# Block products with seven multiplications in the channel mixer of an attention-and-mixer kernel

## The chip, the cores and the metric

The kernel runs on one core of a Trainium2 chip. The core has a matrix engine (TensorE, PE in the profile), a vector engine (VectorE, DVE), a scalar engine (ScalarE, ACT), a general engine (GpSimd, POOL) and a queue engine (SyncE, SP), 16 DMA engines, an on-chip memory of 128 partitions (SBUF) and eight accumulator banks (PSUM). PEld is TensorE's loading of the stationary operand, which overlaps its matmuls. The metric is the device time of one execution in microseconds. Three runs of the kernel before took 810.48, 810.80 and 811.31 us; the median is 810.8.

## What is computed

Eight batches go through attention in chunks of 64 rows and then through a mixer with a token part and a channel part. Cut to what matters:

```python
B, H, S, D = 8, 8, 576, 64                     # chunk = 64
scores = scale * q_c @ k_c.transpose            # 64 x 64 for each of 9 chunks, 8 heads
attn = exp(scores - max) ; attn = attn / (sum(attn) + 1e-9)
x = (attn @ v_c) laid out as (B, 576, 512)
# mixer, for each batch
h = relu(x.T @ w_tok1) @ w_tok2                 # 512 x 576 -> 512 x 256 -> 512 x 576
u = x + h.T
out = u + relu(u @ w_ch1) @ w_ch2               # 576 x 512 -> 576 x 1536 -> 576 x 512
```

All of it is in float32. TensorE takes a rounded form of it (float32r). To keep the precision, every operand is split into a high part (rounded) and a low part (the value less its rounded form), and every product is computed as three: high by high, low by high and high by low (`THREE` in the code).

## The kernel before

The batches are numbered b = 0 to 7. Attention works on tiles of 128 rows (two chunks), 36 in all; a batch with even b has five tiles, one with odd b four (the middle tile of nine is shared by two batches). The mixer works with the channel dimension (512 = 4 blocks of 128, `NDT`) on partitions and the 576 rows of the sequence as two halves of 288 columns (`HALF`), n = 0 and 1. The hidden channels are 12 blocks of 128 (`NFC`).

For one batch the work is:

- `tok1` (L499): the first token product, two blocks of 128 (`NT1`), 14 matmuls of 512 columns each (`tok1_part`, L476). Then relu on ACT (rh, L493) and the low part on DVE (rl, L494).
- `tok2` (L505): the second token product, 2 halves x 4 blocks x 6 = 48 matmuls of 288 columns (L514), each block followed by the addition of x on DVE (L519), the rounding on ACT (L524) and the low part on DVE or POOL (L525).
- `ch1` (L529): the first channel product of a half n and a block f: 4 x 3 = 12 matmuls (L535), then relu on ACT (gh, L544) and the low part on DVE (gl, L545).
- `ch2` (L559): the second channel product of that block, 4 x 3 = 12 matmuls (L575) into four accumulators that stay in PSUM for all 12 blocks. After the last one DVE adds u's high part (L582), POOL its low part (L584), and SP stores the result.
- One attention interruption (`attention`, L747): the scores of one tile and the values of the tile before it, 64 matmuls of 64x64 (`attn_both`, L309 and L321), into one pair of PSUM banks. Then DVE takes the maximum (mx, L282), subtracts (pr, L285), ACT takes exp (L289), DVE transposes (L332), SP sends the result to DRAM and back in another order (far and pf, `far_out` and `far_in`), and ACT copies it (pt, L360) for the next interruption. DVE also sums the rows (L295) and multiplies the values by the reciprocals (x, L400); ACT and POOL split x (xh, xl, L417 and L418); x is transposed and goes through DRAM too (xt), to be added in `tok2`.

The order on TensorE is written out by hand from b = 1 on (`manual_schedule` for the tensor engine): in 24 steps (n, f) `ch1` of a step, then `ch2` of the step before it. `LAST_STEP` and `STRIDE` say in which steps an attention interrupts. On ACT, DVE and POOL a planner orders the instructions with its own costs; SP is in program order. In batch 0 the planner orders TensorE as well: there DVE and ACT turn the weights, which arrive as 64-bit floats, into float32 (`conversion`) and split them, `STEP_FILL` operations a step. The attention of batch 1's four tiles runs in batch 0, in the slots of `STARTS`: the scores of a tile in one slot, its values three slots later, the next tile after that. The scores of batch 2's first tile (tile 9) stand alone at step 0 of batch 1. At the end of batch 0 and of every later one the two blocks of `tok1` for the next batch stand beside the last two `ch2` steps.

PSUM holds four accumulators (`ps_acc`), two banks for `ch1` and `tok1` (`ps_c1`) and one pair for attention (`ps_at`).

## Time and profile before

| what | value |
|---|---|
| median of three runs | 810.8 us |
| the profiled execution, its own time | 810.02 us |
| its span in the profile | 808.2 us |
| TensorE busy | 787.4 us, 97% |
| DVE, ACT, POOL busy | 378.0, 240.7, 118.5 us |
| moved by DMA | 87.96 MB, mean 109 GB/s |
| granted TensorE clock, mean | 0.992 |

Batch 0 ends (the second token product of b = 1 begins) at about 150 us; later batches begin at 247.8, 342.1, 437.7, 532.0, 627.6 and 721.5 us.

How to read the profile: the page gives busy times by engine, then the span in 40 slices of 20.2 us with the busy share in tenths, then the chain of waits that ended last, then groups of instructions by line, engine, operation and tile with their count, busy time and mean duration in ns, and the idle time before them with what ended it. A tile name such as `gl<-ps_c,gh` reads output, then inputs. L545 is line 545 of the kernel before.

### The profile page before, as it was taken

The numbers are of one execution on the slowest core, as the hardware profiler recorded it, in microseconds if no ns is written. First come the engines' busy times: TensorE is split into PE (matmuls) and PEld (weight loads), VectorE is DVE, ScalarE is ACT, GpSimd is POOL, SyncE is SP. The second block draws the span as 40 slices with busy tenths as digits, with TensorE's granted clock in tenths as the row PEclk, the third lists the DMA queues.
The fourth block names the chain that finished last, engine by engine and source line by source line (L and its number), as shares of the span: only waits on it lengthen the run. The fifth ranks groups of instructions, "written<-read, shape, count | busy, mean of one in ns | idle before, by whom it ended". The sixth has DMA issues, their size and how long they took to land.

```text
span 808.2 us, 17939 instructions
## 1 busy us (share of the span) xinstructions
PE 787.4 (97%) x7556; PEld 752.1 (93%) x7556; DVE 378.0 (47%) x799; ACT 240.7 (30%) x496; POOL 118.5 (15%) x137
## 2 busy tenths in 40 slices
PE   7889999899999999999999999999999999999997
PEld 5579989799999999999999999999999999999997
DVE  5989985545344344253534334344533445232111
ACT  4667643322232222132223222222223222121111
POOL 0000120401203021130203102030200302033000
PEclk8999999999999999999999999999999999999999
DMA  9953322344432233123441234222342223200000
GB/s 349 406 190 105 119 79 96 135 122 141 148 112 64 92 122 107 56 79 125 141 151 58 64 115 140 88 70 93 131 145 89 76 88 101 67 30 1 1 30 30
DMA packets 69985, 87.96 MB, mean 109 GB/s; under 512 B 8016, under 2 KB 48208, under 8 KB 69904
## 3 DMA queue, kind: packets, MB, share of 16 engines
q1 hardware_dynamic: 69904, 86.82, 32.5%
q8 instruction: 59, 0.97, 0.5%
q14 instruction: 22, 0.18, 0.1%
HBM read 59.92 MB, written 25.95 MB: 106 GB/s over the span
## 4 chain that ended last, share of the span: by engine, by line
PE 85%; DVE 8%; DMA 3%; ACT 2%; issue 1%; SPq 0%; ACTq 0%; DVEq 0%
PE acc L575 36%; PE ps_c L535 33%; PE ps_t L476 6%; PE ps_t L514 6%; PE ps_sv L309 2%; PE ps_sv L321 2%; DVE wtop L173 1%; DVE wtop L181 1%; DMA xc<-x 1%; DVE kept_c L231 1%; DVE wtop L160 1%; DMA raw_t<-in_w 1%; DMA pf<-far 1%; DVE wtop L166 1%; PE sum L485 0%
## 5 line engine op out<-in xcount | busy, mean ns | idle before, releaser
L535 PE MATMUL ps_c<-uh,kept_c 128*128 128x288 f32 x1536 | 310.8, 295 | 3.4 <-ACT xt L447 1.9
L575 PE MATMUL acc<-gh,kept_c 128*128 128x288 f32 x1536 | 311.9, 299 | 1.6 <-ACT kept_c L225 1.1
L535 PEld LDWEIGHTS ps_c<-uh,kept_c 128*128 128x128 f32 x1536 | 245.8, 188 | 4.8 <-ACT xt L447 2.1
L575 PEld LDWEIGHTS acc<-gh,kept_c 128*128 128x128 f32 x1536 | 244.2, 188 | 6.4 <-ACT kept_c L225 1.8
L535 PE MATMUL ps_c<-ul,kept_c 128*128 128x288 f32 x768 | 226.6, 295 | 0.0
L545 DVE SCALAR_TENSOR_TENSOR gl<-ps_c,gh 128x288 fp32r<-128x288 f32 x180 | 81.4, 452 | 310.1 <-ACT gh L544 309.9
L575 PE MATMUL acc<-gl,kept_c 128*128 128x288 f32 x768 | 219.5, 295 | 0.0
L544 ACT ACTIVATE gh<-ps_c 128x288 fp32r<-128x288 f32 x180 | 74.1, 411 | 317.1 <-PE ps_c L535 316.6
L535 PEld LDWEIGHTS ps_c<-ul,kept_c 128*128 128x128 f32 x768 | 144.2, 188 | 0.1
L575 PEld LDWEIGHTS acc<-gl,kept_c 128*128 128x128 f32 x768 | 142.9, 189 | 0.1
L418 POOL TENSOR_TENSOR xl<-x,xh 128x512 fp32r<-128x512 f32 x28 | 38.3, 1366 | 413.0 <-ACT xh L417 413.0
L584 POOL TENSOR_TENSOR o<-o,ul 128x288 f32<-128x288 f32 x56 | 44.1, 813 | 192.7 <-DVE o L582 191.1
L514 PE MATMUL ps_t<-kept_t,rh 128*128 128x288 f32 x224 | 44.7, 295 | 0.3 <-ACT rh L493 0.3
L289 ACT ACTIVATE pr<-pr 128x512 f32<-128x512 f32 x36 | 22.7, 632 | 61.6 <-DVE pr L285 59.9
L582 DVE TENSOR_TENSOR o<-acc,uh 128x288 f32<-128x288 f32 x56 | 22.7, 448 | 36.1 <-PE acc L575 31.5
L476 PE MATMUL ps_t<-xh,kept_t 128*128 128x512 f32 x112 | 36.0, 405 | 2.5 <-ACT xh L417 2.5
L524 ACT CAST uh<-u 128x288 fp32r<-128x288 f32 x64 | 27.1, 433 | 37.6 <-DVE u L519 37.6
L360 ACT COPY pt<-pf 128x512 f32<-128x512 f32 x31 | 19.2, 620 | 60.3 <-DMA pf<-far 60.3
L514 PEld LDWEIGHTS ps_t<-kept_t,rh 128*128 128x128 f32 x224 | 35.9, 188 | 1.0 <-ACT rh L493 1.0
L514 PE MATMUL ps_t<-kept_t,rl 128*128 128x288 f32 x112 | 33.2, 297 | 0.2 <-DVE rl L494 0.2
L519 DVE TENSOR_TENSOR u<-ps_t,xt 128x288 f32<-128x288 f32 x64 | 28.4, 452 | 9.8 <-PE ps_t L514 9.4
L525 POOL TENSOR_TENSOR ul<-u,uh 128x288 fp32r<-128x288 f32 x35 | 29.1, 848 | 10.0 <-ACT uh L524 9.5
(79 smaller groups left out, 629.4 us busy)
## 6 DMA issues: line engine op xcount, KB each, us to landing
qk<-in_qk SPq DMA_DIRECT2D x36, 512.0 KB, 3.9
far<-blocks SPq DMA_DIRECT2D x63, 256.0 KB, 2.1
raw_c<-in_wc SPq DMA_DIRECT2D x24, 512.0 KB, 9.0
v<-in_v SPq DMA_DIRECT2D x36, 260.0 KB, 4.1
out<-o SPq DMA_DIRECT2D x64, 144.0 KB, 1.9
pf<-far SPq DMA_DIRECT2D x124, 64.0 KB, 2.0
xt<-far SPq DMA_DIRECT2D x112, 64.0 KB, 2.0
raw_t<-in_w SPq DMA_DIRECT2D x4, 288.0 KB, 7.9
```

The source lines that it names most:

```text
L289: nc.scalar.activation(out=pr, in_=pr, func=AF.Exp, scale=1.0 / float(D) ** 0.5)
L418: nc.gpsimd.tensor_tensor(out=xl, in0=t["x"], in1=xh.bitcast(F32), op=ALU.subtract)
L476: nc.tensor.matmul(ps, lhsT=lhsT, rhs=rhs, start=(n == 0 and q == 0), stop=(n == len(mt) - 1 and q == len(terms) - 1),)
L514: nc.tensor.matmul(ps[:, :HALF], lhsT=lhsT[:, m * P:(m + 1) * P], rhs=rhs, start=(k == 0 and q == 0), stop=(k == NT1 - 1 and q == len(term ...
L519: nc.vector.tensor_tensor(out=u.rearrange("p (i c) -> p i c", c=BK), in0=ps[:, :HALF].rearrange("p (i c) -> p i c", c=BK), in1=xt[:, n * H ...
L524: nc.scalar.copy(out=uh[:, m], in_=u)
L525: return lambda engine: engine.tensor_tensor(out=ul[:, m], in0=u, in1=uh[:, m].bitcast(F32), op=ALU.subtract)
L535: nc.tensor.matmul(ps[:, :HALF], lhsT=weights["c1", f][:, wi, k * P:(k + 1) * P], rhs=u[ui][:, k], start=(k == 0 and q == 0), stop=(k == N ...
L544: nc.scalar.activation(out=gh, in_=ps[:, :HALF], func=AF.Relu)
L545: nc.vector.scalar_tensor_tensor(out=gl, in0=ps[:, :HALF], scalar=0.0, in1=gh.bitcast(F32), op0=ALU.max, op1=ALU.subtract)
L575: nc.tensor.matmul(accs[e], lhsT=weights["c2", f][:, wi, e * P:(e + 1) * P], rhs=g[gi], start=(f == 0 and q == 0), stop=(f == NFC - 1 and ...
L584: nc.gpsimd.tensor_tensor(out=o, in0=o, in1=u[1][:, e].bitcast(F32), op=ALU.add)
```

## The change

From b = 2 on the first channel product is no longer computed block by block. Two blocks of hidden channels, two halves of the input channels and two halves of the sequence make a 2x2 by 2x2 block product. It is computed with seven block products in place of eight (Winograd's form of Strassen's method): sums of the weight blocks (S1 to S4) and of the blocks of u (T1 to T4) are multiplied, and the results are sums of the seven products (`seven`). Six such pairs (`NPAIR`) make a batch.

The sums of weights don't change from batch to batch. They are made once in batch 1 (`make`, in the steps `MAKE`), split, and written to DRAM together with the plain blocks (`send`, two steps later). Every pair of every batch from b = 2 on loads its seven blocks from DRAM (`load`), on ACT's DMA queue, in two transfers into doubled buffers. The sums of u are made in each batch from the second token product (`operands`); their high parts come from ACT, their low parts from DVE or, for three of them, POOL.

Both halves of the sequence come out of a pair together. The first half goes into `ch2` at once, in the next pair; the second half is kept in SBUF (`store`) and runs as 12 `ch2` steps when the pairs are done. The first token product of the next batch stands before the last three of these steps (`TOKEN_1`), and the last two steps (`TOKEN_2`) are kept back: one runs after the next batch's second token product, one after the first two products of its first pair.

PSUM: from b = 2 on the banks of `ps_c1` and `ps_at` become one pool of four (`ps_mix`), from which token products, block products and attention all take their tiles in turn. Attention takes two of them, so its DVE operations come in two halves.

The attention of batch 1's tiles in batch 0 also takes the merged form, scores of a tile with values of the tile before, in five slots; tile 9's scores move into the last of them. In batch 1 the attention stands before `ch1`, and the steps are 4, 8, 12, 16 and 20. From b = 2 on it stands where `BREAKS` says. The weights of the token products become slices of two tiles (`wtall` and `kept_t`), and batch 0's kept relu results one tile. The output addition of b = 2 to 7 needs one DVE operation in place of one on DVE and one on POOL, as u is kept whole.

The diff, cut to its core:

```diff
+SEVEN = (
+    ("A11", "B11"), ("A12", "B21"), ("S2", "T2"), ("S1", "T1"), ("S4", "B22"), ("S3", "T3"), ("A22", "T4"),
+)
+GROUP = 4
+NPAIR = NFC // 2
+BREAKS = {
+    5: (("pair", 0), ("pair", 2), ("pair", 4), ("mid", 5), ("step", 4)),
+    4: (("pair", 1), ("pair", 3), ("pair", 5), ("step", 3)),
+}
+TOKEN_1, TOKEN_2 = 8, 10
+LOW_ON_GPSIMD = {"B21", "B22", "T3"}
+MAKE = (1, 5, 9, 13, 17, 20)
+SEND = 2
+FIRST_LOADS = (21, 23)
-LAST_STEP, STRIDE, FIRST_STEP = 19, {5: 4, 4: 5}, 0
+LAST_STEP, STRIDE = 20, 4
-STARTS = ((8, 9, 11, 12), (13, 14, 16, 17), (18, 19, 21, 22), (23, 24, 26, 27))
+STARTS = (10, 14, 18, 22, 26)
...
+    def tok1_pair(b, cover):
+        src, tag = (ps_mix[0], "c") if mixing else (ps_c1, "c1")
+        ps = []
+        for m in range(NT1):
+            ps.append(src.tile([P, 512], F32, tag=tag, name="ps_t1"))
+            for n in range(NKT - 1):
+                tok1_part(b, m, n, ps[m])
+            if m == 0:
+                cover()
+        for m in range(NT1):
+            tok1_part(b, m, NKT - 1, ps[m])
+        return [tok1_end(x) for x in ps]
...
+    def make(p):
+        full = pool.tile([P, 2, DM], F32, tag="full", name="full", bufs=1)
+        for i in range(2):
+            w = weights["c1", 2 * p + i]
+            nc.gpsimd.tensor_tensor(
+                out=full[:, i], in0=w[:, 0].bitcast(F32), in1=w[:, 1].bitcast(F32), op=ALU.add
+            )
...
+        for i, x, op, y in (
+            (1, a21, ALU.add, a22), (0, sums[:, 1], ALU.subtract, a11),
+            (2, a12, ALU.subtract, sums[:, 0]), (3, a11, ALU.subtract, a21),
+        ):
+            nc.vector.tensor_tensor(out=sums[:, i], in0=x, in1=y, op=op)
+        parts = pool.tile([P, 4, 2, DM // 2], F32R, tag="wparts", name="wparts", bufs=1)
+        nc.scalar.copy(out=parts[:, :, 0], in_=sums)
+        nc.vector.tensor_tensor(
+            out=parts[:, :, 1], in0=sums, in1=parts[:, :, 0].bitcast(F32), op=ALU.subtract
+        )
+        return parts
+    def send(p, parts):
...
+        for at, src in ((0, a1[:, 0]), (1, a1[:, 1]), (slice(2, 6), parts.bitcast(F32)), (6, a2[:, 1])):
+            nc.scalar.dma_start(out=mixed[p][:, at], in_=src)
+    def load():
+        if loads:
+            src = mixed[loads.pop(0)]
+            got = []
+            for tag, lo, hi in (("mwa", 0, GROUP), ("mwb", GROUP, len(SEVEN))):
+                w = pool.tile([P, hi - lo, 2, DM // 2], F32R, tag=tag, name=tag)
+                nc.scalar.dma_start(out=w.bitcast(F32), in_=src[:, lo:hi])
+                got += [w[:, i] for i in range(hi - lo)]
+            loaded.append(got)
...
+    def operands(b, r):
...
+        def add(name, src):
+            full[name] = src
+            high, low = [every[:, len(ops), i] for i in range(2)]
+            nc.scalar.copy(out=high, in_=src)
+            engine = nc.gpsimd if name in LOW_ON_GPSIMD else nc.vector
+            engine.tensor_tensor(out=low, in0=src, in1=high.bitcast(F32), op=ALU.subtract)
+            ops[name] = (high, low)
+        def minus(name, x, y):
+            t = pool.tile([P, 2, HALF], F32, tag="diff", name="diff", bufs=2)
+            nc.vector.tensor_tensor(out=t, in0=full[x], in1=full[y], op=ALU.subtract)
+            add(name, t)
...
+        minus("T2", "B22", "T1")
+        minus("T3", "B22", "B12")
+        minus("T4", "B21", "T2")
+    def seven(p, ops, w, store, between, interrupt):
+        def run(i):
+            ps = ps_mix[0].tile([P, 512], F32, tag="c", name="ps_m")[:, :HALF]
+            for k in range(2):
+                for q, (wi, ui) in enumerate(THREE):
+                    nc.tensor.matmul(
+                        ps, lhsT=w[i][:, wi, k * P:(k + 1) * P], rhs=ops[SEVEN[i][1]][ui][:, k],
+                        start=(k == 0 and q == 0), stop=(k == 1 and q == 2),
+                    )
+            return ps
+        m1 = half("m1")
+        nc.scalar.copy(out=m1, in_=run(0))
+        first = relu_split(plus(half("c11"), run(1), m1))
+        interrupt("mid", p)
+        between(0)
+        u2 = plus(half("u2"), run(2), m1)
+        u4 = plus(half("u4"), run(3), u2)
+        between(1)
+        plus(store[:, 2 * p], run(4), u4)
+        m7 = run(5)
+        u3 = plus(half("u3"), m7, u2)
+        plus(store[:, 2 * p + 1], m7, u4)
+        second = relu_split(plus(half("c21"), run(6), u3))
+        return first, second
...
+    for b in range(2, B):
+        u, ops = operands(b, r)
+        rest.pop(0)()
...
+        def between(k):
+            if todo:
+                ch2(b, 0, u[0], *todo[k], accs)
+            elif k == 0:
+                rest.pop(0)()
+        for p in range(NPAIR):
+            interrupt("pair", p)
+            first, second = seven(p, ops, loaded.pop(0), store, between, interrupt)
+            load()
+            todo = [(2 * p, first), (2 * p + 1, second)]
+        for f, g in todo:
+            ch2(b, 0, u[0], f, g, accs)
+        accs, ahead, rest = [], relu_split(store[:, 0]), []
+        for f in range(NFC):
+            interrupt("step", f)
+            g, ahead = ahead, None
+            if b + 1 < B and f >= TOKEN_2:
+                g = g or relu_split(store[:, f])
+                rest.append(lambda b=b, f=f, g=g, u=u[1], accs=accs: ch2(b, 1, u, f, g, accs))
+            else:
+                if b + 1 < B and f == TOKEN_1:
+                    r = tok1_pair(b + 1, lambda: ch2(b, 1, u[1], f, g, accs))
+                else:
+                    ch2(b, 1, u[1], f, g, accs)
+                ahead = relu_split(store[:, f + 1]) if f + 1 < NFC else None
```

`half` takes a buffer of 288 columns, `plus` adds a PSUM tile and an SBUF tile on DVE, and `relu_split` takes relu on ACT (high part) and the low part on DVE.

More of the change, by code (lines that the diff above doesn't have):

```diff
@@ L120, in attention_mixer_kernel @@
     plan += [(("t2", k, n), w2_in, k * S + n * HALF, HALF) for n in range(2) for k in range(NT1)]
-    token = len(plan)
+    token, token_words = len(plan), sum(p[3] for p in plan)
     for f in range(-1, NFC):
@@ L222, in split_high @@
         name = "kept_" + "_".join(map(str, key))
-        kept = ctx.enter_context(tc.tile_pool(name=name, bufs=1, reuse_waits="tile"))
-        parts = tops[key, "parts"] = kept.tile([P, 2, n], F32R, name=name)
+        if i < token:
+            if "kept_t" not in weights:
+                weights["kept_t"] = const.tile([P, 2 * token_words + 2 * DT], F32R, name="kept_t")
+            at = 2 * sum(p[3] for p in plan[:i])
+            parts = weights["kept_t"][:, at:at + 2 * n].rearrange("p (w n) -> p w n", w=2)
+        else:
+            kept = ctx.enter_context(tc.tile_pool(name=name, bufs=1, reuse_waits="tile"))
+            parts = kept.tile([P, 2, n], F32R, name=name)
+        tops[key, "parts"] = parts
         nc.scalar.copy(out=parts[:, 0], in_=tops[i])
@@ L301, in attn_both @@
     def attn_both(i, j):
-        ps = ps_at.tile([P, 2, 512], F32, tag="at", name="ps_sv")
+        if mixing:
+            ps = [ps_mix[0].tile([P, 512], F32, tag="c", name="ps_sv") for _ in range(2)]
+        else:
+            pair = ps_at.tile([P, 2, 512], F32, tag="at", name="ps_sv")
+            ps = [pair[:, a] for a in range(2)]
         if i is not None:
@@ new lines, in make @@
+    def make(p):
[5 more added lines that the diff above has]
+            )
+        (a11, a12), (a21, a22) = [[full[:, i, h * DM // 2:(h + 1) * DM // 2] for h in range(2)] for i in range(2)]
+        sums = pool.tile([P, 4, DM // 2], F32, tag="wsum", name="wsum", bufs=1)
+        for i, x, op, y in (
[5 more added lines that the diff above has]
+        nc.scalar.copy(out=parts[:, :, 0], in_=sums)
+        nc.vector.tensor_tensor(
+            out=parts[:, :, 1], in0=sums, in1=parts[:, :, 0].bitcast(F32), op=ALU.subtract
+        )
+        return parts
@@ new lines, in later @@
+    def later(job, *args):
+        with tc.issue_after([i for i in nc.cur_bb.bb.instructions if i.engine == nc.scalar.engine][-1]):
+            job(*args)
+    done = len(STARTS)
+    us = []
+    for n in range(2):
+        uh = pool.tile([P, NDT, HALF], F32R, tag="uh", name="uh")
+        ul = pool.tile([P, NDT, HALF], F32R, tag="ul", name="ul")
+        us.append((uh, ul))
+        for m in range(NDT):
+            tok2(1, r, n, m, us[n])(nc.vector if n * NDT + m in UL_ON_VECTOR else nc.gpsimd)
@@ new lines, in attention_mixer_kernel @@
+    ends = len(batch_tiles(2))
+    steps = {LAST_STEP - STRIDE * k for k in range(ends)}
+    made, pend = [], None
+    for n in range(2):
+        accs = []
+        for f in range(NFC):
+            step = n * NFC + f
+            if step in steps:
+                attention(done)
+                done += 1
+            g = ch1(us[n], f)
+            if step in MAKE:
+                with ExitStack() as late:
+                    newest = {i.engine: i for i in nc.cur_bb.bb.instructions}
+                    for engine in (nc.scalar.engine, nc.vector.engine):
+                        late.enter_context(tc.issue_after(newest[engine]))
+                    made.append((step + SEND, MAKE.index(step), make(MAKE.index(step))))
+            if made and made[0][0] == step:
+                later(send, *made.pop(0)[1:])
+            if step in FIRST_LOADS:
+                later(load)
+            if step == 2 * NFC - 2:
+                held = pend
+            elif step == 2 * NFC - 1:
+                rest = [pend, (1, n, us[n], f, g, accs)]
+                r = tok1_pair(2, lambda: None)
+                ch2(*held)
+            elif pend is not None:
+                ch2(*pend)
+            pend = (1, n, us[n], f, g, accs)
@@ new lines, in half, with plus, relu_split @@
+    def half(name, bufs=2):
+        return pool.tile([P, HALF], F32, tag=name, name=name, bufs=bufs)
+    def plus(dst, ps, other):
+        nc.vector.tensor_tensor(out=dst, in0=ps, in1=other, op=ALU.add)
+        return dst
+    def relu_split(src):
+        gh, gl = g_parts()
+        nc.scalar.activation(out=gh, in_=src, func=AF.Relu)
+        nc.vector.scalar_tensor_tensor(
+            out=gl, in0=src, scalar=0.0, in1=gh.bitcast(F32), op0=ALU.max, op1=ALU.subtract
+        )
+        return gh, gl
```

237 lines of the change are left out of this document (127 added, 110 removed).

## The prediction

> **What bounds the kernel now.** I read the page first, then the windows by stage, then what TensorE waited for.
>
> ```profile
> span 808.2 us, 17939 instructions
> PE 787.4 (97%) x7556; PEld 752.1 (93%) x7556; DVE 378.0 (47%) x799; ACT 240.7 (30%) x496; POOL 118.5 (15%) x137
> DVE  5989985545344344253534334344533445232111
> ```
> ```profile
> 60.00:80.00 20.00, 20.00 (x173) 19.31 (x172) 20.00 (x43) 15.20 (x30) 0.00 (x0) 1.00 0.31 106
> 247.80:342.10 94.30, 94.30 (x910) 92.11 (x910) 36.70 (x78) 21.87 (x46) 15.55 (x18) 1.00 0.30 93
> 342.10:437.70 95.60, 95.60 (x975) 93.19 (x974) 42.34 (x88) 25.44 (x52) 15.65 (x18) 1.00 0.35 112
> ```
> ```profile
> PE ps_sv L321 <- ACT pt L360: 0.5, 1, 0.5
> PE ps_t L514 <- ACT rh L493: 0.3, 1, 0.3
> PE ps_t L514 <- DVE rl L494: 0.2, 1, 0.2
> ```
>
> In a window row the columns are PE, PEld, DVE, ACT and POOL busy, granted clock, DMA share and GB/s. The batches called b = 2 and b = 3 in the code (windows two and three) keep TensorE busy for all of their 94.3 and 95.6 us, DVE for 37 to 42. The three waits are all that TensorE had on other engines from 150 us on: 1.0 us. Busy PE alone doesn't prove a bound, but without waits the time of these stages is the number of matmuls times their pace. Batch 0 is another stage: there DVE is full as well (20.00 of 20 us), because it converts weights.
>
> **The pace**, from the chain of waits (start, us, what):
>
> ```profile
> 247.80 6.33 PE ps_t L514 x48
> 254.13 3.19 PE ps_c L535 x24
> ...
> 332.39 3.26 PE ps_t L476 x14
> ```
> ```profile
> 354.82 1.60 PE acc L575 x12
> 356.42 1.57 PE ps_c L535 x12
> 357.99 0.62 PE ps_sv L309 x32
> 358.62 0.47 PE ps_sv L321 x32
> 359.09 1.79 PE acc L575 x12
> ```
>
> 24 first-channel matmuls take 3.19 us: 0.133 us each. A second-channel step (12) takes 1.60, the 48 of the second token product 6.33, the 14 wider ones (512 columns) of half a first token product 3.26, 0.233 each. An attention interruption holds the stream from 357.99 to 359.09 and slows the next step by 0.19: 1.10 + 0.19 = 1.3 us.
>
> **1. Seven products for eight, b = 2 to 7.** Before, one batch needs 2 halves x 12 blocks x 4 k x 3 terms = 288 first-channel matmuls of 288 columns. After, it needs 6 pairs x 7 products x 2 k x 3 terms = 252 of the same shape. 36 fewer x 0.133 = 4.79 us a batch, x 6 = **-28.7 us**. All of it lies on the path, as TensorE has no other wait there. The second-channel and token products stay the same in number.
>
> **2. Attention merged in batch 0 and 1.** Before, the four tiles of batch 1 have scores and values in two interruptions each, and tile 9's scores stand alone in batch 1. After, five merged ones in batch 0 and five in batch 1. TensorE saves about two gaps of 0.3 us in the part where it is the bound: **-0.6 us** (-1.5 to 0). The DMAs of an attention (out, back, the next loads) move with it on SP's queue, which there carries only the output stores beside them.
>
> **3. The end of batch 0.**
>
> ```profile
> 144.00:146.50 2.50, 0.04 (x4) 0.00 (x0) 2.33 (x6) 0.62 (x1) 2.50 (x4) 0.97 0.01 3
> 146.50:150.40 3.90, 3.48 (x8) 2.15 (x8) 0.72 (x3) 1.09 (x2) 1.43 (x2) 0.58 0.29 100
> ```
> ```profile
> 143.34 0.70 PE L379 MATMUL ps_v<-v,pt 64*64 64x65 f32 x32
> 146.53 2.08 PE L476 MATMUL ps_t<-xh,kept_t 128*128 128x512 f32 x4 [2.49 <-ACT xh L417]
> 148.40 1.06 PE L476 MATMUL ps_t<-xl,kept_t 128*128 128x512 f32 x2
> 149.72 0.55 PE L514 MATMUL ps_t<-kept_t,rh 128*128 128x288 f32 x2 [0.26 <-ACT rh L493]
> 150.44 0.40 PE L514 MATMUL ps_t<-kept_t,rl 128*128 128x288 f32 x1 [0.18 <-DVE rl L494]
> ```
>
> The values of the last tile come only at 143.34, so the token product waits 2.49 us for its xh, then runs at a granted clock of 0.58, and the second token product gets both its operands only at 150.44. From 144.04, six matmuls of 0.233 us would end at 145.4: some 4.9 us are lost. After, scores of tile k+1 come with values of tile k, so four chains follow each other with no value stage between, and the last tile should be done well before; tok1_pair also puts a second-channel step behind both ends. What is late next is DVE: up to 115 us it is full, the change puts a row sum a tile (L295, 0.64 us, quoted in part 6; before, a column of ones gave it) and another tile's maximum, subtraction and transposition (2.1 us) ahead of the last weight conversions. I count 4.4 us there (about 3.5 tiles), one for one. Together **-0.5 us** (-5 if the added DVE work finds room, +5 if the tail stays and the work is added).
>
> **4. Making and sending the sums, in batch 1.** Six times: two POOL additions (L418's 1.37 us each), four 256-wide and one 1024-wide DVE operations (about 2.7 us by the rows below), an ACT copy of about 1.1, four DMA issues on ACT. Cover: ch1's result is needed one ch1 and one ch2 later, 3.2 us, of which 411 + 452 ns are the split. 2.2 us of room against bursts of 2.7: **+1 us** (0 to +4). The issues stand ahead of the next relu on ACT.
>
> **5. Loading the blocks.**
>
> ```profile
> 20.00:42.00 22.00, 17.62 (x184) 10.60 (x184) 19.57 (x49) 14.84 (x30) 0.00 (x0) 1.00 1.03 407
> ```
> ```profile
> qk<-in_qk SPq DMA_DIRECT2D x36, 512.0 KB, 3.9
> raw_c<-in_wc SPq DMA_DIRECT2D x24, 512.0 KB, 9.0
> ```
>
> A pair is 7 x 2 x 256 x 4 B x 128 = 1.84 MB, two DMAs. TensorE spends 42 x 0.133 + 2 x 1.60 = 8.8 us on a pair, so 209 GB/s, with some 90 for attention: 300, under the 407 that this core moved. The load goes out after pair p for pair p+2, so 8 to 10 us to land: between the 3.9 (quiet) and 9.0 us (a full queue) of the rows, nearer the quiet one in this stage. Cost taken: 0 (0 to +24, rival D). The wait for a free buffer stands on ACT's queue, ahead of the relu of the next pair.
>
> **6. The new chain of vector work: what hides it.**
>
> ```profile
> L545 DVE SCALAR_TENSOR_TENSOR gl<-ps_c,gh 128x288 fp32r<-128x288 f32 x180 | 81.4, 452 | 310.1 <-ACT gh L544 309.9
> L544 ACT ACTIVATE gh<-ps_c 128x288 fp32r<-128x288 f32 x180 | 74.1, 411 | 317.1 <-PE ps_c L535 316.6
> L418 POOL TENSOR_TENSOR xl<-x,xh 128x512 fp32r<-128x512 f32 x28 | 38.3, 1366 | 413.0 <-ACT xh L417 413.0
> L360 ACT COPY pt<-pf 128x512 f32<-128x512 f32 x31 | 19.2, 620 | 60.3 <-DMA pf<-far 60.3
> ```
> ```profile
> 359.15 0.69 DVE L282 TENSOR_REDUCE mx<-ps_sv 128x8 f32<-128x512 f32 x1 [0.22 <-PE ps_sv L321]
> 359.88 0.69 DVE L285 TENSOR_TENSOR pr<-ps_sv,mx 128x512 f32<-128x512 f32 x1
> 360.49 0.68 DVE L400 TENSOR_TENSOR x<-ps_sv,zs 128x512 f32<-128x512 f32 x1
> 361.27 0.71 DVE L332 STREAM_TRANSPOSE blocks<-pr 128x512 f32<-128x512 f32 x1
> 361.91 0.64 DVE L295 TENSOR_REDUCE zs<-pr 128x8 f32<-128x512 f32 x1
> 362.47 0.70 DVE L332 STREAM_TRANSPOSE blocks<-x 128x512 f32<-128x512 f32 x1
> ```
>
> A pair gives DVE seven additions and two splits of about 0.45 us, 4.05 of its 8.8. An attention adds some 5.0 (the rows above, now in halves, and the reciprocal): 9.05 of 10.1. So DVE is nearly full in pairs with attention, and half idle in the others. Each product takes one of four PSUM banks and holds it until DVE or ACT has read it; each fifth product needs the first one's bank, so DVE may lag about 2.4 us before TensorE feels it. After an attention, the third product needs the bank of its first half 3.2 us after its end (two products 1.6, a step 1.6). DVE's order of before (mx, pr, x, then the transpositions) frees it after about 2.5. Cover holds, with 0.7 to spare.
>
> The tight place is the first pair of a batch. Estimates for 576-wide work from the rows of 288 and 512: DVE 0.75, ACT 0.68, POOL 1.5 us. From the start of the second token product: it ends at 6.3, the kept step at 7.9, two products at 9.5, the other kept step at 11.1, then products three (operand T2) to seven (T4, at 14.3). The last u is added at 6.8; T2 is split by 9.0, in time. POOL's three low parts (B21, B22, T3) run from 6.3 to 10.9; T4 finds a free diff buffer (two of them) then, and is subtracted, rounded and split by 13.1. But between 6.8 and 13.1 DVE also has four output additions, two additions and one split of the pair and another sum: 7.35 us of work for 6.3. I take 0.5 us of stall for b = 2, 4, 6, 7. For b = 3 and 5 an attention stands right there: 5.0 us of DVE for 1.3 of TensorE, of which 2.4 can be put off: 2 us each. The last pair's second block needs addition, relu and split (1.5 us and hand-offs) behind one step of 1.60: inside the 0.5. The first token product moves from the end of a batch to before its last three steps; its relu and split (0.6 and 0.7 us) lie behind the ninth step's 1.60, at no cost; without that cover it would be 1.3 us a batch. Sum **+6 us** (0 to +18).
>
> For the upper end, rows of DVE and POOL beside each other:
>
> ```profile
> 250.49 2.58 POOL L525 TENSOR_TENSOR ul<-u,uh 128x288 fp32r<-128x288 f32 x3
> ```
> ```profile
> 251.37 1.03 DVE L525 TENSOR_TENSOR ul<-u,uh 128x288 fp32r<-128x288 f32 x1
> 253.27 0.46 DVE L525 TENSOR_TENSOR ul<-u,uh 128x288 fp32r<-128x288 f32 x1
> ```
>
> The same DVE subtraction takes 1.03 us while POOL works and 0.46 when it is idle. [...]
>
> **Sum.** The profiled execution took 810.0 us (span 808.2 and 1.8 around it), the median of the three runs is 810.8. From 810.0: -28.7 - 0.6 - 0.5 + 1 + 6 = 787.2; from the median **788.0 us**. 0.2% is 1.6 us, about what a measurement can tell.
>
> **Rivals.**
> A, everything is covered and the tail of batch 0 comes back: 810.8 - 28.7 - 0.6 - 4.9 = 776.6. For: DVE averages under 75% of the new batch. Against: the bursts of part 6.
> [...]
> C, slower: DVE puts the x product behind exp, transposition and row sums (the order in which the code lists them). Then the bank comes 4.2 to 5 us after the attention instead of 2.5, against 3.2 of cover: 1.6 us at each of 22 attentions, +35: 823. It loses from 1.04 us an attention on (22.8 / 22). Against: the order in the rows above.
> D, the blocks land late, as raw_c's 9.0 us would make them: 1 us for each of 24 pairs (third to sixth of six batches): 812. Against: the DMA share of 0.30 in this stage.
>
> **How the numbers follow.** Forecast 0.50 (781 to 795), A 0.22, B 0.18, C 0.06, D 0.04. Faster: forecast, A, B and a bit of D, 0.91; same 0.02; slower 0.07. The range 776 to 802 leaves out C, most of D and the edges of A and B.
>
> **What would show it.** Right: 252 product matmuls a batch at 0.133 us; batches of about 90 us; TensorE's waits on DVE in the first pair of b = 3 and 5; tile 8's values well before 138 us. Wrong: TensorE waiting for DMA at a pair's first product (D), for PSUM at a pair's third product (C), waits of over 2 us in every first pair (B), batch 0 ending later than 155 us, or a granted clock under 1.00 after 160 us.

## The result, and the profile after

The kernel after took 847.5 us (median of four runs, 843.7 to 857.1) beside 810.6 for the kernel before: a ratio of 1.0439, 95% interval 1.0391 to 1.0487. It is slower by 4.4%; 788 was forecast. Ratios, here and below, leave out runs over 1.5% above the fastest of their kernel; the profiled execution of the kernel after is such a run (857.1 us), so single batches of its profile come out long, by some 10 us in all against the median.

The page of the kernel after: engines, three rows of the 40 slices, and the two DMA queues that carry data (packets, MB, share of 16 engines' span; q1 is SP's, q10 ACT's).

```profile
PE 786.8 (92%) x7340; PEld 742.9 (87%) x7340; DVE 531.8 (62%) x1179; ACT 256.7 (30%) x532; POOL 103.8 (12%) x89
DVE  5899994666536664485555866465646665738451
PEclk7999999999988999999999999999989999999999
DMA  9944333467792887247863588516866188723611
q1 hardware_dynamic: 69904, 86.82, 30.9%
q10 hardware_dynamic: 16128, 77.08, 26.5%
```

DVE went from 47 to 62% and is no bound yet. The 216 matmuls saved are there (7340 for 7556), but TensorE, idle for 21 of 808 us before, now stands idle for 68 of 855. ACT's queue moves 77 MB that weren't there. What SP's transfers take from issue to landing (median us, last column), before and after:

```profile
far<-blocks SPq DMA_DIRECT2D x63, 256.0 KB, 2.1
pf<-far SPq DMA_DIRECT2D x124, 64.0 KB, 2.0
```
```profile
qk<-in_qk SPq DMA_DIRECT2D x36, 512.0 KB, 5.2
far<-blocks SPq DMA_DIRECT2D x63, 256.0 KB, 3.1
pf<-far SPq DMA_DIRECT2D x124, 64.0 KB, 2.6
```

All three are later; qk took 3.9 before. These medians mix in batch 0, where no block is loaded. In the window 250 to 770 us of the kernel after, where loads run, the same two transfers take nearly twice as long as before (2.1 and 2.0 also in that window of the kernel before):

```profile
far<-blocks SPq DMA_DIRECT2D x43, 256.0 KB, 3.9
pf<-far SPq DMA_DIRECT2D x84, 64.0 KB, 3.7
```

Split by whether a block load was on its way when the transfer was issued (from the issue and landing times of this trace), pf took 4.0 us in the median beside a load (68 issues) and 1.9 without one (16); far took 4.5 and 2.2. The windows by batch of the kernel after (b = 1, 2, 5 and 7; columns as in the prediction) show the granted clock under 1.00 and, in all but the last batch, a DMA share of about 0.6, where it was 0.30 to 0.35 in the prediction's rows:

```profile
148.90:256.60 107.70, 97.29 (x950) 93.39 (x949) 61.04 (x117) 29.94 (x58) 31.31 (x27) 0.96 0.68 233
256.60:359.80 103.20, 95.19 (x875) 92.01 (x874) 60.40 (x136) 23.74 (x51) 13.74 (x11) 0.94 0.61 200
...
564.20:672.00 107.80, 96.95 (x939) 92.87 (x938) 63.13 (x149) 27.01 (x57) 9.99 (x7) 0.95 0.61 196
...
767.80:851.10 83.30, 81.94 (x614) 81.10 (x612) 43.17 (x93) 15.71 (x37) 4.81 (x3) 1.00 0.32 103
```

And this is what TensorE waited for in the kernel after (total us, times, longest); before, all its waits on other engines from 150 us on came to 1.0 us:

```profile
PE ps_m L989 <- DVE u L971: 11.9, 7, 4.2
PE ps_m L989 <- DVE every L932: 10.2, 6, 2.9
PE acc L640 <- ACT gh L976: 9.0, 3, 3.7
PE ps_sv L371 <- ACT pt L412: 7.0, 3, 5.2
PE ps_t L532 <- DVE stack L490: 5.5, 1, 5.5
```

No line names a DMA, so by this view alone DVE and ACT look slow. The timeline of the kernel after, just ahead of an interruption of b = 3, shows what stands behind the first of these lines:

```profile
405.47 1.75 SPq L395 DMA_DIRECT2D pf<-far  x4
405.55 0.96 PE L989 MATMUL ps_m<-every,mwb 128*128 128x288 f32 x6
...
408.80 0.62 ACT L412 COPY pt<-pf 128x512 f32<-128x512 f32 x1 [7.90 <-DMA pf<-far]
...
409.33 0.44 ACT L976 ACTIVATE gh<-c 128x288 fp32r<-128x288 f32 x1
...
409.80 0.46 DVE L977 SCALAR_TENSOR_TENSOR gl<-c,gh 128x288 fp32r<-128x288 f32 x1 [8.32 <-ACT gh L976]
410.17 0.45 DVE L971 TENSOR_TENSOR u<-ps_m,m 128x288 f32<-128x288 f32 x1
...
410.68 1.63 PE L989 MATMUL ps_m<-every,mwb 128*128 128x288 f32 x8 [4.17 <-DVE u L971]
```

Read it from the bottom. The pair's sixth product (the fifth is the row at 405.55) waits 4.17 us until DVE's u has read the third out of its PSUM bank; u stands in DVE's order behind gl, gl needs gh, and gh stands in ACT's order behind the copy pt, which had waited 7.90 us for pf. Here one late transfer held two engines that work in order, and TensorE after them. From b = 2 on TensorE has nine waits of over 1.2 us on u, gh or pt, 25.8 us in all. Behind each of them, in the same way, is a pt that had waited for pf, 1.5 us in one case and 5.4 to 7.9 in the others. Where the issue of a block load stands between this copy and the relu, it took 0.33 us, within the copy's own time.

After this wait the granted clock was lower as well. The windows behind it (columns as above) show 0.50 for 3.4 us:

```profile
411.50:414.90 3.40, 3.40 (x72) 3.12 (x71) 1.99 (x5) 0.44 (x1) 0.00 (x0) 0.50 1.05 307
414.90:418.30 3.40, 3.40 (x36) 3.33 (x29) 3.13 (x9) 1.75 (x4) 0.13 (x1) 1.00 1.02 384
```

From 256.6 us on, the clock record of this trace has seven stretches at 0.50, of 3.4 or 6.8 us each. All seven begin during a wait of TensorE of 1.8 to 5.2 us on DVE or ACT, or within 1 us of its end; behind four other waits, of 1.5 to 2.5 us (ending at 378.1, 614.7, 708.0 and 729.6), there is none.

### The profile page after: what moved, and what is told of

It is laid out like the page before. It is cut to its first block, busy times and chain, and to the rows that moved or that the text cites. A ratio compares the mean times of both kernels' runs of the same rounds, so it can differ in the third digit from the quotient of the medians.

```text
span 855.2 us, 18102 instructions
## 1 busy us (share of the span) xinstructions
PE 786.8 (92%) x7340; PEld 742.9 (87%) x7340; DVE 531.8 (62%) x1179; ACT 256.7 (30%) x532; POOL 103.8 (12%) x89
## 3 DMA queue, kind: packets, MB, share of 16 engines
q10 hardware_dynamic: 16128, 77.08, 26.5%
## 5 line engine op out<-in xcount | busy, mean ns | idle before, releaser
L989 PE MATMUL ps_m<-every,mwa 128*128 128x288 f32 x864 | 132.6, 302 | 5.5 <-DVE every L932 2.9
L989 PEld LDWEIGHTS ps_m<-every,mwa 128*128 128x128 f32 x864 | 121.5, 192 | 8.1 <-DVE every L932 3.1
L989 PE MATMUL ps_m<-every,mwb 128*128 128x288 f32 x648 | 98.5, 302 | 20.6 <-DVE u L971 11.9
L989 PEld LDWEIGHTS ps_m<-every,mwb 128*128 128x128 f32 x648 | 90.7, 192 | 24.2 <-DVE u L971 13.6
L976 ACT ACTIVATE gh<-c 128x288 fp32r<-128x288 f32 x72 | 31.9, 443 | 181.9 <-DVE c L971 148.8
L605 PE MATMUL ps_c<-uh,kept_c 128*128 128x288 f32 x384 | 80.5, 301 | 3.2 <-ACT xt L503 2.1
L977 DVE SCALAR_TENSOR_TENSOR gl<-c,gh 128x288 fp32r<-128x288 f32 x72 | 32.8, 455 | 79.9 <-ACT gh L976 79.2
L605 PEld LDWEIGHTS ps_c<-uh,kept_c 128*128 128x128 f32 x384 | 61.9, 189 | 4.8 <-ACT xt L503 2.3
L605 PE MATMUL ps_c<-ul,kept_c 128*128 128x288 f32 x192 | 56.9, 298 | 0.0
L412 ACT COPY pt<-pf 128x512 f32<-128x512 f32 x31 | 19.2, 619 | 111.4 <-DMA pf<-far 106.1
L333 ACT ACTIVATE pr<-pr 128x512 f32<-128x512 f32 x36 | 22.7, 631 | 72.5 <-DVE pr L328 53.4
L971 DVE TENSOR_TENSOR u<-ps_m,u 128x288 f32<-128x288 f32 x72 | 32.6, 455 | 12.5 <-PE ps_m L989 10.6
L605 PEld LDWEIGHTS ps_c<-ul,kept_c 128*128 128x128 f32 x192 | 36.3, 189 | 0.1
```

What stands on the lines that cost most here:

```text
L333: nc.scalar.activation(out=pr, in_=pr, func=AF.Exp, scale=1.0 / float(D) ** 0.5)
L412: nc.scalar.copy(out=pt.rearrange("p (h i q) -> p i h q", i=4, q=BK), in_=pf,)
L605: nc.tensor.matmul(ps[:, :HALF], lhsT=weights["c1", f][:, wi, k * P:(k + 1) * P], rhs=u[ui][:, k], start=(k == 0 and q == 0), stop=(k == N ...
L971: nc.vector.tensor_tensor(out=dst, in0=ps, in1=other, op=ALU.add)
L976: nc.scalar.activation(out=gh, in_=src, func=AF.Relu)
L977: nc.vector.scalar_tensor_tensor(out=gl, in0=src, scalar=0.0, in1=gh.bitcast(F32), op0=ALU.max, op1=ALU.subtract)
```

## The experiments

Theory T: the block traffic, and the issuing of the sends, make other transfers late, and that is the loss. Rival V: the new vector work, operand stage and bank hand-offs are the loss. D is rival D of the prediction (the blocks themselves land late). All ratios are to runs of the kernel before on the same chip (medians 810.0 to 811.5). The batches are those of one profiled execution each. The durations are worked out from the starts of the second token products in the matmul records of each profile:

| run | median us | ratio | b=0 ends | b=1 | 2 | 3 | 4 | 5 | 6 | 7 |
|---|---|---|---|---|---|---|---|---|---|---|
| before | 810.6 | 1 | 149.7 | 97.9 | 94.3 | 95.6 | 94.3 | 95.6 | 93.8 | 82.8 |
| after | 847.5 | 1.0439 | 148.9 | 107.8 | 103.1 | 106.2 | 98.3 | 107.8 | 95.8 | 83.3 |
| e1_no_reload | 812.2 | 1.0028 | 148.8 | 105.5 | 97.0 | 95.0 | 91.1 | 93.5 | 90.9 | 82.9 |
| e5_few_sends | 800.6 | 0.9868 | 148.8 | 97.2 | 94.9 | 94.9 | 91.0 | 93.4 | 90.5 | 83.0 |
| e11_even | 848.9 | 1.0441 | 150.9 | 106.4 | 103.7 | 105.4 | 96.0 | 106.7 | 91.3 | 83.3 |
| e12_sums_only | 823.7 | 1.0154 | 151.3 | 95.9 | 98.2 | 100.4 | 94.0 | 100.3 | 95.8 | 84.0 |
| e18_sums_two_deep | 824.7 | 1.0174 | 161.4 | 96.2 | 94.3 | 96.8 | 93.9 | 97.4 | 92.9 | 85.5 |
| e22_sums_two_deep_late | 813.9 | 1.0046 | 150.7 | 97.2 | 94.5 | 97.5 | 95.4 | 97.9 | 93.0 | 85.8 |
| e23_two_deep_late | 845.3 | 1.0436 | 148.3 | 108.3 | 97.7 | 103.7 | 96.9 | 104.6 | 95.9 | 83.3 |

From before to after two second-channel steps (3.2 us) move from the end of each batch into the next, so before's 97.9 and 82.8 compare with 94.7 and 86.0 there.

### Take the traffic away, or add it to the kernel before

**e1_no_reload.** After two pairs no weights are loaded any more:

```diff
+            if len(loaded_all) >= 2:
+                loaded.append(loaded_all[p % 2])
+                return
```

> The changed kernel, but only the first two pairs of blocks are loaded and used for all pairs (the products of the other pairs are so of wrong weights; everything else is issued as before). Theory T (traffic): block loads double attention's way through DRAM, the copy of pt waits for it in ACT's queue with the relus behind it. Then far and pf land in about 2 us again, ACT's wait for pf falls from 106 us to some 60, batches b = 2 to 6 lose their gaps of 3 to 5 us, and the time falls from 847 to about 815 (batch 1 is unchanged). Theory V (vector work: bursts of DVE, banks, the operand stage): the time stays within 840 to 850. Rival D (blocks late): about 840, as no gap stands at a pair's first product.

Measured: 812.2 (interval of the ratio 1.0005 to 1.0052). 35 us of the loss are gone, with every product and every vector operation still in place: V falls as the main cause. In the window 250 to 720 us far and pf land in 2.1 and 2.0 us again, as T expected. The total wait of pt for pf did not fall as expected (113.5 us, 106.1 in the kernel after), as ACT often has nothing else to do meanwhile; only what is queued behind it counts. Windows of the run, b = 2 and b = 5, against those above:

```profile
254.30:351.30 97.00, 92.31 (x874) 89.13 (x873) 60.32 (x136) 23.59 (x51) 13.78 (x11) 0.98 0.33 101
...
537.40:630.90 93.50, 91.20 (x938) 88.57 (x937) 63.46 (x149) 27.13 (x57) 10.02 (x7) 1.00 0.35 108
```

DVE has the same 60 and 63 us of work in a batch that is 6 and 14 us shorter.

**e5_few_sends.** As e1, and only two of the six pairs are sent.

> e1 without the sends of four of the six pairs (the sums are still made). Theory T: batch 1 falls from 108 us to about 98, as ACT's queue is no longer held by the DMA issues, the whole about 805. Theory V: the make stage is dear for its DVE work, so batch 1 stays at 105 to 108 and the time equals e1's.

Measured: 800.6 (0.9842 to 0.9895). Batch 1 goes from 105.5 to 97.2. This is what the change is worth with little of its traffic left (two pairs are still sent and loaded): 10 us.

**e4_before_traffic.** The kernel before, with spare copies on ACT's queue:

```diff
+    def traffic():
+        for _ in range(2):
...
+            nc.scalar.dma_start(out=copy, in_=qk_in[i:i + 2].rearrange("t p c -> p t c"))
...
+                if b > 1 and (n * NFC + f) % 3 == 0 and n * NFC + f < 18:
...
+                        traffic()
```

> The kernel before with the traffic alone: from b = 2 on, at every third of the first 18 steps, two copies of 1.05 MB from DRAM to DRAM on ACT's queue, which nobody waits for. Theory T: far and pf take 3 to 5 us each in place of 2, ACT's wait for pf passes 100 us, and the time rises to 820 to 850. Theory V: 811 to 814, as the vector work is that of before.

Measured: 867.9, ratio 1.0708 (1.0688 to 1.0727), more than T expected. The copies put 75.5 MB on ACT's queue, for 77.1 in the kernel after, and none of the change's vector work is in this kernel. In the window 250 to 770 us pf takes 5.6 us and far 4.9. The wait below came to 0.5 us from 150 us on without the copies:

```profile
PE ps_sv L321 <- ACT pt L360: 39.2, 13, 6.6
```

**e2_pt_on_pool.** The copy pt moves from ACT to POOL.

> The changed kernel with the copy of pt on POOL in place of ACT, so that its wait for pf holds no relu. Theory T: the gaps ahead of gh and c go, 815 to 830; what is left is the values' own wait for pt. Theory V: 843 to 852, POOL gets work and its low parts come later.

Measured: 855.1, ratio 1.0524 (1.0480 to 1.0569): missed. Batch 0 ends 8 us later, for a reason left open (the copy is not slower: 613 ns in the median, 619 on ACT, though one took 5.0 us), and TensorE waits for pt itself, 5.9 and 6.1 us at a time. That freeing the relus helps little while the product with the values, in TensorE's own order, waits for the same transfer is argued from these waits; the 8 us hide a part.

### Is it the size of the packets, the issuing engine, or the place of the interruptions?

**e6_small_packets, e7_before_small.** Rows of the DRAM copy get 16 unused numbers, so the bytes go as runs of 1 KB (76800 packets on ACT's queue for 16128); the same for the copies added to the kernel before.

```diff
-    mixed = [dram.tile([P, len(SEVEN), 2, DM // 2], F32, ...
+    mixed = [dram.tile([P, len(SEVEN), 2, DM // 2 + 16], F32, ...
```

> Each row of 256 numbers in the DRAM copy of the weights is followed by 16 unused ones, so the same bytes go and come as packets of 1 KB and not of 4 and 8 KB. Theory R (the sixteen DMA engines turn from one queue to the next after each packet, so that every 512-byte packet of the attention's way back waits for an 8 KB packet of the block loads): the way back (pf) lands in a median near 2 us again, hardly one over 4, and the batches 2 to 6 lose at most 2 us each against the run without traffic: about 822, between 812 and 832. Theory by bytes (the two queues share the bandwidth, whatever the packets): pf as late as in the changed kernel, 843 to 860. [...]

> The kernel before with the same 2.1 MB of spare copies in every third step as in the run that took 868 us, but cut into packets of 1 KB (and twice as many DMA issues). Theory R (turns by packet): the way back is delayed by little, and the time falls from 868 to between 812 and 835. Theory by bytes: 860 to 875. Theory V (vector work and banks; traffic is harmless): it has fallen with the run of large packets and expects nothing of its own here.

Measured: 846.7, ratio 1.0429 (1.0370 to 1.0488), and 869.3, 1.0704 (1.0678 to 1.0730): no change. Theory R's times, 812 to 832 and 812 to 835, were missed; in e6 the small transfers land even later (medians of the whole run, 3.1 and 2.6 in the kernel after):

```profile
far<-blocks SPq DMA_DIRECT2D x63, 256.0 KB, 3.8
pf<-far SPq DMA_DIRECT2D x124, 64.0 KB, 3.8
```

Why they land later stays open. The block queue's share of the DMA engines' time went from 26.5% in the kernel after to 29.6% in e6, and that of the copies from 25.0% in e4 to 28.1% in e7, for the same bytes.

**e10_sends_sp.** The sends are issued by SP in place of ACT.

> The sends of the sums in batch 1 are issued by SyncE and not by ScalarE; nothing else differs from the changed kernel. If what batch 1 loses is ScalarE's time in issuing them (up to 4.9 us a time, with relus behind): batch 1 falls from 107.8 to about 99, and the time to about 839. If it is the transfers themselves that delay the attention of batch 1: batch 1 stays near 108, or rises, as SyncE's queue now carries both, and the time stays between 845 and 855.

Measured: 859.5, ratio 1.0542 (1.0507 to 1.0577). Batch 1 rises to 115.9: SP's queue now holds the last tile's way back, and TensorE waits 13.5 us for it at the end of the batch (ACT's copy of it waits 16.0 for pf).

**e11_even.** The five interruptions of b = 3 and 5 are spaced evenly.

> In batches 3 and 5 the five interruptions are spaced more evenly (pair 0, the middle of pair 1, the start of pair 3, pair 5, step 4, for pair 0, pair 2, pair 4, pair 5, step 4): the least distance grows from about 10 to about 14 us, so that each way through DRAM has more time; nothing else differs from the changed kernel. If the loss comes mainly where an interruption follows the last one by 10 us: batches 3 and 5 fall from 106 and 108 to about 98 to 100, and the time to about 833. If transpositions and relus are late wherever they meet a load: the waits move to other places and the time stays within 840 to 855.

Measured: 848.9 (1.0394 to 1.0488): the waits move to other places, batches 3 and 5 stay at 105.4 and 106.7.

### What batch 1 pays for

The timeline of the kernel after in batch 1 shows ACT's own DMA issues (ACTq) ahead of exp:

```profile
209.66 0.36 ACTq L850 DMA_DIRECT2D mix<-wparts  x1
210.04 4.89 ACTq L850 DMA_DIRECT2D mix<-kept_c  x3
...
214.99 0.63 ACT L333 ACTIVATE pr<-pr 128x512 f32<-128x512 f32 x1 [5.49 <-DVE x L454]
```

The sums (contiguous, one DMA) are issued in 0.36 us. The three block DMAs hold ACT for 4.89, and the note in brackets blames DVE for it. But not all of it is issuing: by their records the three issues take 0.46, 0.78 and 0.37 us. The third starts only at 214.57; it waits on a semaphore that one of SP's xt<-far transfers, issued at 209.79, shares with it, and that transfer landed at 214.55. So a late transfer holds ACT here too. Over batch 1 one issue took (ns: least, median, longest):

```profile
L850 ACTq DMA_DIRECT2D mix<-kept_c x18: 366/618/1502, 165.4 to 247.3; - x18
L850 ACTq DMA_DIRECT2D mix<-wparts x6: 338/346/365, 165.0 to 246.7; - x6
```

Two runs send one kind each for the last four pairs, on top of e1:

**e20_sums_sent, e21_blocks_sent.**

> As the run without the loads of the later pairs (the weights of the first two pairs serve for all, so the products are of wrong weights), and of the pairs 2 to 5 only the sums are sent in batch 1 (one DMA of 1.05 MB each), not the blocks. If the three DMAs of the blocks, with ScalarE held by their issue, are what the sends cost: batch 1 is 97 to 99 us (105.5 with all sends, 97.2 with two of six) and the time about 803. If the bytes are: batch 1 is 101 to 103, as the sums are 0.57 of them, and the time about 807.

> The counterpart: of the pairs 2 to 5 only the blocks are sent (three DMAs, 0.79 MB), not the sums; else as the run beside it. If the issue of the three DMAs is the cost: batch 1 is 103 to 106 and the time about 810. If the bytes are: batch 1 is 100 to 101 and the time about 804.

Measured: 805.5 (0.9927 to 0.9954), batch 1 101.6; and 803.7 (0.9906 to 0.9952), batch 1 103.1. The sums alone come out as the bytes would have them; for the blocks alone batch 1 fits the issue and the whole time the bytes. Against e5 the sums of four pairs (4.2 MB) cost 4.4 us in batch 1 and 4.9 in the whole time, the blocks (3.1 MB) 5.9 and 3.1. So neither kind is clearly dearer by the byte, and how the loss of batch 1 divides between bytes and issues stays open.

**e16_two_deep_early, e17_sums_only_early.** Sums made at steps 1 to 16, on top of e14 and e12 below (in e16 the first loads come earlier as well).

> As the run with the product two interruptions after the scores, and in batch 1 the sums are made at steps 1, 4, 7, 10, 13, 16 (for 1, 5, 9, 13, 17, 20) and the first two pairs loaded at steps 18 and 21 (for 21 and 23), so that the last sends and the first loads don't meet the way of the last tile before batch 2. If what batch 1 loses lies at its end (a wait of 5.6 us there in the changed kernel): batch 1 falls by 4 to 6 us and the time is about 811. If it lies in ScalarE's issuing wherever a send stands: batch 1 is the same within 2 us, and the time that of the run beside it.

> As the run that sends and loads the sums alone, with the sums made at steps 1, 4, 7, 10, 13, 16 (the loads at 21 and 23 as they were). If the end of batch 1 is where its loss lies, batch 1 falls by 1 to 4 us against the run beside it; otherwise the same within 1 us.

Measured: 855.0 (ratio 1.0498, 1.0428 to 1.0568) and 829.6 (1.0228, 1.0196 to 1.0260). Batch 1 gets longer by 4 and 5 us (111.5 and 100.7); in e16 the wait at its end shrinks from 6.0 to 2.7, and others take its place. Both expectations missed.

### Fewer bytes, or more time for the way

**e12_sums_only.** A11, A12 and A22 are read where batch 1 has them; only the four sums of a pair are sent, in one DMA, and loaded, in four, into the six A21 places.

```diff
+        nc.scalar.dma_start(out=mixed[p], in_=parts.bitcast(F32))
...
+    a21 = [weights["c1", 2 * p + 1][:, :, :DM // 2] for p in range(NPAIR)]
+    ring = a21
...
+                nc.scalar.dma_start(out=slot.bitcast(F32), in_=mixed[p][:, i])
```

> The blocks A11, A12 and A22 are read from where batch 1 has them in SBUF; only the four sums of a pair are sent and loaded, 1.05 MB for 1.84 MB a pair, into the places of the six A21 blocks, two DMAs in the middle of a pair and two at its end (some SBUF tiles are cut into smaller ones, or have one buffer for two, to make room). Theory T: the time lost to traffic falls at least with the bytes, to 0.57 or less: batch 1 from 107.8 to about 102, batches 2 to 6 by half of what they lose against the run without loads, in all about 822, between 812 and 832. If the loss is by the number of transfers or by their collision with the interruptions, whatever their size: 838 or more.

Measured: 823.7 (1.0118 to 1.0191), as T expected. Batch 1 falls by 12 us, further than expected: the block DMAs are gone, and the first loads bring 1.6 MB for 3.7. ACT issues 144 loads here for 72 and is held by them for longer (56.5 us of issuing, 25.6 in the kernel after), yet the kernel is 24 us faster; so the issuing of the loads is not the main loss. Landing times (whole run) and TensorE's first wait of this run:

```profile
far<-blocks SPq DMA_DIRECT2D x63, 256.0 KB, 2.3
pf<-far SPq DMA_DIRECT2D x124, 64.0 KB, 2.8
```
```profile
PE acc L640 <- ACT gh L988: 11.7, 7, 3.0
```

**e14_two_deep, e19_two_deep_mended, e23_two_deep_late.** All the traffic, but the values of a tile are multiplied two interruptions after its scores. One interruption more is needed at the start: e14 puts it into batch 0 ahead of the others, e19 between them, e23 into step 1 of batch 1. The edit of e14 and e19 (e23 counts scores and values apart):

```diff
-        j = order[k - 1] if k else None
+        j = order[k - 2] if k > 1 else None
...
-        t["pf"] = pool.tile(..., tag="pf", name="pf", bufs=1)
+        t["pf"] = pool.tile(..., tag="pf", name="pf", bufs=2)
```

> The changed kernel with all its traffic, but the product with the values of a tile is taken not at the next interruption after its scores but at the one after that, so that the way through DRAM has twice the time (a second buffer for what comes back, and the values loaded one interruption later). Theory T (the traffic costs time only because the attention's way through DRAM comes back too late for the next interruption): TensorE's waits for pt and ScalarE's wait for pf (102 to 125 us in all in the runs with traffic) go almost to nothing, batches 2 to 6 come down to within 1 or 2 us of the run without the loads (97, 95, 91, 94, 91), batch 1 keeps its sends, and the time is about 816, between 808 and 824. If the traffic slows something else too (VectorE or ScalarE in SBUF, TensorE's own reads, or the other transfers): the waits for pt go and the time stays above 830.

> All the traffic of the changed kernel, the product two interruptions after the scores, and the interruptions of batch 0 at slots 10, 13, 16, 19, 22, 26 (the run before had 8, 10, 14, ... and ended batch 0 14 us later, which hid what it gained). T: batch 0 ends within 2 us of the changed kernel's 148.9, the batches behind it last as in that run (107.7, 96.9, 102.6, 91.7, 104.2, 95.9, 83.4), in all about 837, between 830 and 842. If its gain in batches 2 to 6 came from batch 0's shift and not from the longer time of the way: 845 or more.

> All the traffic of the changed kernel, and from batch 1 on the product with the values two interruptions after the scores, with the one more at step 1 of batch 1; batch 0 is the changed kernel's. T: batch 0 ends near 149, batch 1 lasts 108 to 110, batches 2 to 7 as in the two runs with the product later (96.9 to 99, 101 to 102.6, 91.7 to 93, 102.7 to 104.2, 96 to 97, 83.4): about 836, between 830 and 842, for 847.5. If twice the time for the way through DRAM is worth nothing by itself: 845 or more.

Measured: 850.8 (ratio 1.0495, 1.0467 to 1.0523), 852.5 (1.0521, 1.0493 to 1.0548) and 845.3 (1.0418 to 1.0454). In e14 and e19 batch 0 ends at 163.0 and 161.0: an interruption more costs 12 to 14 us where DVE is full, at both places tried. e23 is clean of that, and T in its narrow form (only pt comes late) falls: TensorE's waits of ps_sv for pt fall from 7.0 to 0.6 us, and the time is that of the kernel after. The waits of e23:

```profile
PE ps_m L997 <- DVE every L940: 18.5, 7, 5.1
PE ps_t L532 <- DVE stack L490: 8.4, 2, 5.6
PE ps_m L997 <- ACT m L1004: 4.5, 2, 3.9
```

The longest of them, in its timeline:

```profile
470.11 1.84 SPq L650 DMA_DIRECT2D out<-o  x4
...
477.45 0.46 DVE L979 TENSOR_TENSOR store<-ps_m,u 128x288 f32<-128x288 f32 x1 [4.27 <-DMA out<-o]
477.83 0.75 DVE L940 TENSOR_TENSOR every<-diff,every 128x576 fp32r<-128x576 f32 x1
...
478.63 1.33 PE L997 MATMUL ps_m<-every,mwb 128*128 128x288 f32 x4 [5.08 <-DVE every L940]
```

Now the late transfer is the output of the batch before: DVE waits 4.27 us for out<-o, which has nothing to do with store but, it seems, its place in SBUF (that they share one is inferred from the wait). By the trace's landing times the first two of the four stores, issued before ACT's block load of 471.04, took 1.8 and 1.9 us, the other two 6.2 and 5.7. With one late transfer out of the way the next takes its place.

**e18_sums_two_deep, e22_sums_two_deep_late.** Both remedies, with the extra interruption in batch 0 and in batch 1.

> The two partial remedies together: only the sums are sent and loaded (1.05 for 1.84 MB a pair, the blocks read where they lie), and the product with the values comes two interruptions after the scores; the one interruption more in batch 0 stands between the others (slots 10, 13, 16, 19, 22, 26) and not ahead of them. Theory T (transfers made late by the traffic, and ScalarE's issuing of the block sends, are the whole loss): batch 1 near 96, batches 2 to 6 near 97, 96, 91.5, 96, 92, the last 84, batch 0 up to 2 us later: about 807, between 801 and 814, so as fast as the kernel before or faster. If a good part of the loss is something that the traffic slows beside the transfers' lateness: 817 or more.

> Only the sums are sent and loaded, and from batch 1 on the product with the values comes two interruptions after the scores: the one interruption more (scores alone) stands at step 1 of batch 1, and batch 0 has the changed kernel's five. T: batch 0 ends near 151 as in the run with the sums alone, batch 1 lasts 97 to 99, the batches behind it as in the run with both remedies (94.3, 96.8, 93.9, 97.4, 92.9, 85.5): about 813, between 807 and 817. If the time gained behind batch 1 in that run came only from what batch 0 lost: 821 or more.

Measured: 824.7 (1.0146 to 1.0202), over the 801 to 814 that T expected, with batch 0 12 us late as in e19; and 813.9 (1.0029 to 1.0062), as expected. Here twice the time for the way is worth 10 us against e12, where under the full traffic it was worth nothing. It is the best version with the whole computation, and still behind the kernel before by 0.3 to 0.6%. In batches 2 to 6 it lacks 13.5 us to e5.

Not tried: one sum more kept in SBUF, the sends or the loads on POOL's queue, and the low parts of the operands taken off POOL. The loads also stand in ACT's order; e1 takes that away together with the bytes, and no run separates the two. The nine waits above and e12's issues speak for the bytes.

## Why the prediction was wrong

By differences of medians, the 59.5 us between 788.0 and 847.5 come apart into 12.6 (to e5), 11.7 (the other four sends, e5 to e1) and 35.3 (the loads of all later pairs, e1 to after).

**Part 5 is the step that failed: "Cost taken: 0".** It set 300 GB/s against the 407 that the core had moved, and asked only whether the blocks would be there in time. They were: no wait of TensorE on the blocks is among the lines. What it didn't ask is what a share of 0.6 does to the transfers already there. These are small and on the path, and each interruption counted on them: beside a load pf took 4.0 us for 1.9, and the loads of the later pairs cost 35.3 us where 0 was taken. Its range "0 to +24" was of rival D, whose mechanism was not seen, and was too short as well. The sign that came true, a granted clock under 1.00 after 160 us (0.94 to 0.98 in batches 1 to 5), was named without a mechanism.

**Part 4 had the place and missed the size.** "The issues stand ahead of the next relu on ACT" was named and not priced: +1 us (0 to +4) for batch 1. From 94.7 it went to 105.5 with all sends (e1) and 97.2 with two of six (e5).

**Part 1 and part 6 together were 11 us too good.** Against before, e5's batches 2 to 7 stand at +0.6, -0.7, -3.3, -2.2, -3.3 and -3.0 (the last against 86.0): -11.9 where -28.7 + 6 = -22.7 was forecast. The 36 matmuls a batch are gone and the pace of 0.133 us holds within a run of matmuls (in the kernel after, 30 block-product matmuls from 791.44 us take 3.99). TensorE's idle time in these six batches of e5 is 9.1 us (2.2, 2.3, 0.8, 2.3, 0.8 and 0.8) where 6 of stall were forecast; the stalls in the first pairs of b = 3 and 5 are 2.3 us each in e5 and in the kernel after, near the 2 forecast. So idle time explains 3 of the 11 us. The rest lies within TensorE's busy time; two stretches of 3.4 us at a granted clock of 0.50 (from 264.7 and 360.3 us; the mean of these two batches is 0.98) make an estimated 3.4 of it, at half the pace, and some 4 stay open. In the operand stage the four T subtractions (duration in ns: least, median, longest; lines of e5) took up to 1.99 us each, where 0.75 was estimated:

```profile
L945 DVE TENSOR_TENSOR diff<-base x12: 746/1365/1987, 251.9 to 719.6; 128x576 f32<-128x576 f32 x12
L945 DVE TENSOR_TENSOR diff<-base,diff x12: 740/1248/1559, 254.5 to 724.4; 128x576 f32<-128x576 f32 x12
```

In e5's trace the 11 of the 24 that no POOL instruction overlaps took 0.74 to 0.75 us, the 13 that one overlaps 1.00 to 1.99; against 0.75 these add 12.3 us of DVE's time. But rival B's sign, waits of over 2 us in every first pair, was seen in b = 3 and 5, where the forecast had them too, and in b = 2 in pieces. What the overlap costs TensorE is not shown, as no run took the work off POOL; so no run shows the upper end of part 6, +18, and what e5 shows in its place is the 9.1 us of idle time.

**Parts 2 and 3 held.** Batch 0 ends at 148.9, 0.8 us earlier; -1.1 was forecast. The values of the last tile stand at 128 us, and TensorE is busy without a break from 115 us to the end of the batch. e14, e18 and e19 show how near the edge that was: one interruption more there costs 12 us.

**Rival C's sign was seen without C.** TensorE did wait for a PSUM bank inside a pair (at the sixth product, not the third), but DVE's order was not the reason: DVE was held by ACT, and ACT by pf.

## What to carry to other kernels

Before trading arithmetic for traffic, add the traffic alone to the old kernel: e4 would have shown the loss in one run, without any of the change. Average bandwidth was no cover here (300 GB/s estimated, 407 moved before); list the small transfers that engines wait for in order, and ask how much later each may come. And under the full traffic more slack for one of them bought nothing (e23 845.3, the kernel after 847.5); with fewer bytes it bought 10 us (e22 813.9, e12 823.7).

## What was not expected of the hardware

A second queue at 26% of the DMA engines' time put the 256 KB store from 2.1 to 3.1 us and the 512 KB load from 3.9 to 5.2 over the whole run, and the store to 3.9 where the loads run; cutting its runs from 6 and 8 KB to 1 KB did not help (3.8 for the store in e6). The tails are worse than the medians: in the stretch shown above all four pf issues were out by 407.2, and ACT got its data at 408.8 after 7.90 us of standing. The issue of one DMA with a strided source held ACT for 0.37 to 1.50 us, against 0.34 to 0.37 for a contiguous one of four times the bytes. And the batches grew by more than TensorE's gaps: in e23 batches 2 to 6 have 22 us more of gaps than in e1 but are 31 us longer, at a granted clock of 0.95 to 0.98 where e1 has 0.98 to 1.00.
